# Routed experts with their remainders in halves and quarters of a block: nineteen blocks a phase instead of twenty

## The chip, the cores and the metric

The kernel runs on one core of a Trainium2 chip. The core has five engines that run side by side and meet through semaphores: TensorE (PE; its weight loads are shown apart as PEld), VectorE (DVE), ScalarE (ACT), GpSimd (POOL) and SyncE (SP), which here issues transfers. Sixteen DMA engines move data between the main memory, the on-chip memory (SBUF) and within it. TensorE writes its results to PSUM. The metric is the device time of one execution in microseconds (us), the median of several.

## The reference

Four batches of eight attention heads, whose queries are averaged in pairs, give 4 x 576 = 2304 tokens of 512 numbers. Each token goes to one of eight experts, which is a product with `w1[e]` (512 x 1024), a clip at zero, a product with `w2[e]` (1024 x 512) and a factor `p[e]`:

```python
scores = scale * np.matmul(q.reshape(B, H, S // 2, 2, D).mean(axis=3), k.transpose(0, 1, 3, 2))
attn = np.exp(scores - np.max(scores, axis=-1, keepdims=True))
x = np.matmul(attn / (np.sum(attn, axis=-1, keepdims=True) + 1e-09), v)      # then (4, 576, 512)
logits = np.einsum('bsd,de->bse', x, w_gate)
local_gate = 1.0 / (1.0 + np.exp(-np.einsum('bsd,de->bse', x, w_local).squeeze(-1)))
for s in range(S):
    fresh_e = int(np.argmax(logits[b, s]))
    e = fresh_e if s == 0 or local_gate[b, s] < 0.5 else prev_e
    prev_e = e
    h = np.maximum(x[b, s] @ w1[e], 0.0)
    out[b, s] = p[e] * (h @ w2[e])           # p: softmax of logits[b, s]
```

How many tokens an expert gets is known only when the kernel runs. With these inputs the eight experts get 192, 447, 145, 124, 34, 656, 132 and 574 tokens, which is 15 full blocks of 128 and remainders of 64, 63, 17, 124, 34, 16, 4 and 62.

## The kernel before

Attention runs in 288 steps (32 heads of nine key tiles). Behind it the last batch's tokens are routed, and then the experts run.

**Blocks.** Tokens are sorted into blocks of 128 with one expert each. There are `NST` = 20 block places `j`. An expert's remainder of more than 64 tokens takes a full block; remainders of up to 64 share the four places in `PAIRS` = (7, 11, 15, 19), two to a place, each in half of its 128 columns. A branch at the end (`tail`, L1390 on) runs further blocks where the full ones don't fit; with these inputs it is not entered.

**Phases.** All numbers are split into a high and a low float16 part, so each product is three matmuls. The weights are too large to be held at once in this form, so the experts run in eight phases of 20 blocks. An even phase multiplies every block by a quarter of `w1` (`mm1`, L1077 and `block1`, L1220: 24 matmuls of 128 columns with the weights as stationary operand; a pair takes 48 of 64 columns). An odd phase multiplies by the matching quarter of `w2` (`mm2`, L1129 and `block2`, L1231: six matmuls of 512 columns with the block as stationary operand; a pair takes twelve, two side by side in the two halves of the output). `psh` and `pso` are the outputs of the two in PSUM; ScalarE and VectorE take `hq` from `psh` (L1081, L1082), and VectorE adds `pso` to `acc` (L1144). In phase 7 each finished `acc` is written out by GpSimd with an indirect transfer (`scatter`, L1235).

**Weights.** While a phase runs, the weights of the next are loaded in 16 pieces `c` (`w_load`, L589, on SP's queue), rounded to the high part by ScalarE (`w_hi`, L594), and the low part is made by VectorE (`w_lo`, L600). The place where each piece stands in the program is a step `j` of the phase: load at `14c // 15`, high part three steps later, low part four. The first four pieces of phase 1 have buffers of their own (`we`) and are loaded at the four steps that follow attention's last.

**Copies.** In an even phase the expert's weights must be copied to a fixed place before TensorE can use them, since the expert number is a register (`copy`, L1062; L1072). VectorE makes most copies (`wc`, three buffers); those in `DMAC` are made by a transfer on SP's queue (`wd`, three buffers): eight in each even phase from phase 2 on, and the four second halves in each odd phase.

**Routing.** `gate_ops` and `route_ops` (L887 on) work out on VectorE which token stands where (`s1` to `s9`); a set of small matmuls (L940, L942) turns this into a token list `gid` per block. From `gid` GpSimd gathers the blocks' rows. The first six blocks hold tokens of the first three batches, and their work is written by hand between the routing's steps (`PLAN`).

All engines run their instructions in the order written (`manual_schedule`); SP's queue too waits at its first instruction whose buffer isn't free.

Of the kernel before, what the change touches and what calls it, by code (L numbers as in the profile page):

```python
# [448 lines left out]
NBLK = 25  # L449
NST = 20  # L450
PAIRS = (7, 11, 15, 19)
NFULL = NST - len(PAIRS)
NCOL = NBLK + len(PAIRS)
PST = slice(PAIRS[0], NST, 4)
NG = 20
# [8 lines left out]
NWD = 3  # L464
NWS = 3
NE = 4
RV = (3, 4)
# [5 lines left out]
DMAC = {5: 0, 7: 1, 9: 0, 11: 1, 13: 0, 15: 1, 17: 0, 19: 1}  # L473
NA = 14
# [5 lines left out]
def consts():  # L480
# [7 lines left out]
    full = [j for j in range(NBLK) if j not in PAIRS]  # L488
    key = np.zeros(NCOL)
    key[full] = np.arange(len(full))  # L490
    key[list(PAIRS) + list(range(NBLK, NCOL))] = len(full) + np.arange(2 * len(PAIRS))
    a[:, 384:384 + NCOL] = key[None]
    c["c16"] = a
    f = np.zeros((128, 113), np.float32)
    f[:, 0:8] = 8 - np.arange(8)
    f[:, 8:16] = np.arange(8)
    f[:, 16:32] = 1
    f[:, 24] = 0
    f[:, 34:59] = np.where(np.isin(np.arange(NBLK), PAIRS), 99, key[:NBLK])
    f[:, 60:85] = 4000 + np.arange(128)[:, None] * 25 + np.arange(25)[None]  # L500
# [23 lines left out]
class Moe:  # L524
    def __init__(self, tc, ctx, cc, io, out):
# [12 lines left out]
        self.c32 = per.tile([128, 113], F32, name="c32")  # L538
# [12 lines left out]
        self.eji = per.tile([128, NCOL], I32, name="eji")  # L551
# [3 lines left out]
        self.wcp, self.gx, self.ej, self.sl, self.ep, self.es = {}, {}, {}, {}, {}, {}  # L555
# [3 lines left out]
        self.ejf = per.tile([128, NCOL], F32, name="ejf")  # L559
# [43 lines left out]
    def gate_ops(self, b, XR, xT, sml, psum, ptag, wide):  # L603
# [185 lines left out]
        if last:  # L789
            early = [lambda: [tr(t, 6) for t in range(5)]]  # L790
            s1, s2, s3, s4, s5, s6, s7, s8, s9 = self.route_ops()
            rest = [lambda: (store(0, 512), logits(2, 3)), lambda: tr_pe(3, 0), lambda: tr_pe(3, 1), lambda: logits(3, 4), seq(tok0, o1a), r0_, lambda: o3a(0, 5), e8_, o1e, o2, seq(r1_, p1a), lambda: o3b(0, 5),
                    p1b, p1d, nop, o5, o6, s1, o6b, o7, s2, nop, p1e, s3, o7c, s4, o7d, s5, o8, s6, s7, lambda: s8(psum, ptag), s9]
            return early, lambda: logits(0, 2), rest
# [6 lines left out]
    def full_ops(self, sml, psum, ptag):  # L801
# [9 lines left out]
        def a1():  # L811
            w = self.wst.tile([128, 512], F32, name="wf", tag="wf")
            o = 0
            for k, c in (("fi", 8), ("ff", 8), ("en", 8), ("bs", 8), ("sj", n * 8), ("fs", n), ("js", n), ("m", n), ("om", n), ("ge", 200), ("e1", 25)):
                st[k] = w[:, o:o + c]
                o += c
# [45 lines left out]
        def a12():  # L862
            bj = [128, NBLK, 8]
            V.tensor_tensor(out=st["ge"], in0=c32[:, 34:59].unsqueeze(2).to_broadcast(bj), in1=st["en"].unsqueeze(1).to_broadcast(bj), op=ALU.is_ge)
# [13 lines left out]
    def route_ops(self):  # L878
# [8 lines left out]
        def s1():  # L887
# [6 lines left out]
            st["ni"], st["en"] = w[:, 216:232].bitcast(I32), w[:, 232:248]  # L894
            st["s3"] = w[:, 248:308].rearrange("p (g v) -> p g v", v=3)
            st["jf"], st["c"] = w[:, 308:328], w[:, 328:348]
            V.tensor_scalar(out=st["ni"][:, 0:8], in0=self.cy, scalar1=63.0, scalar2=None, op0=ALU.add)
            V.tensor_scalar(out=st["ni"][:, 8:16], in0=self.cy, scalar1=127.0, scalar2=None, op0=ALU.add)

        def s2():  # L900
            V.tensor_scalar(out=st["ni"], in0=st["ni"], scalar1=7, scalar2=None, op0=ALU.arith_shift_right)
            V.tensor_copy(st["vec"][:, 8:24], st["ni"])
            V.tensor_tensor(out=st["vec"][:, 16:24], in0=st["vec"][:, 16:24], in1=st["vec"][:, 8:16], op=ALU.subtract)

        def s3():
            V.tensor_tensor_scan(out=st["en"], data0=c32[:, 16:32], data1=st["vec"][:, 8:24], initial=self.F, op0=ALU.mult, op1=ALU.add)

        def s4():
            v, en = st["vec"], st["en"]
            V.tensor_tensor(out=v[:, 0:8], in0=en[:, 0:8], in1=v[:, 8:16], op=ALU.subtract)  # L910
            V.scalar_tensor_tensor(out=v[:, 16:24], in0=en[:, 8:16], scalar=float(NBLK - len(PAIRS)), in1=v[:, 16:24], op0=ALU.add, op1=ALU.subtract)
            V.tensor_tensor(out=v[:, 16:24], in0=v[:, 16:24], in1=en[:, 0:8], op=ALU.subtract)
# [15 lines left out]
        def s8(psum, ptag):  # L928
            jj, jf, en, w = st["jj"], st["jf"], st["en"], st["w2"]
            pi = st["pi"] = psum.tile([128, 512], F32, name="pi", tag=ptag)  # L930
            hg = NG // 2
            bg, bh, bj, be = [128, NG, nc_], [128, hg, nc_], [128, n, 8], [128, 8, 8]
            p2 = pi[:, 0:2 * n].rearrange("p (k j) -> p k j", k=2)
            V.tensor_tensor(out=jj[:, :, 0], in0=jf.unsqueeze(2).to_broadcast(bg), in1=c16[:, 384 + NF:384 + NCOL].unsqueeze(1).to_broadcast(bg), op=ALU.is_equal)
            for h in (1, 0):
                g = slice(h * hg, h * hg + hg)
                V.tensor_tensor(out=jj[:, g, 1], in0=jj[:, g, 0], in1=c32[:, 93 + h * hg:93 + h * hg + hg].unsqueeze(2).to_broadcast(bh), op=ALU.mult)
            for h in (1, 0):
                for g in range(h * hg, h * hg + hg):
                    T.matmul(p2, self.R[:, g], jj[:, g, :, 0:n], start=(g == hg), stop=False, skip_group_check=True)  # L940
                for g in range(h * hg, h * hg + hg):
                    T.matmul(p2[64:128, :, PAIRS[0] - NF:NST - NF:4], self.R[:, g, 0:64], jj[:, g, :, n:nc_], start=False, stop=(g == hg - 1), skip_group_check=True)  # L942
            ge, ej = w[:, 0:8 * n].rearrange("p (j e) -> p j e", e=8), self.ejf[:, NF:NBLK]
            gh, eh = w[:, 152:216].rearrange("p (j e) -> p j e", e=8), st["c"][:, 0:8]
            V.tensor_tensor(out=ge, in0=c32[:, 34 + NF:59].unsqueeze(2).to_broadcast(bj), in1=en[:, 0:8].unsqueeze(1).to_broadcast(bj), op=ALU.is_ge)
# [462 lines left out]
```

## Time and profile before

| | |
|---|---|
| median of 3 runs | 670.61 us (669.42 to 671.48) |
| the profiled execution | 671.53 us, of it 669.7 us from its first to its last instruction |
| PE, PEld busy | 644.1 us (96%), 499.6 us (75%) |
| DVE, ACT, POOL busy | 539.3 us (81%), 427.7 us (64%), 425.4 us (64%) |
| attention with the gate of the first batches | to 410 us |
| routing, first blocks and phase 0 | 410 to 471.7 us |
| phases 1 to 7 | 471.7 to 660.1 us |
| last outputs | to 669.7 us |

A busy TensorE is not one at its peak, since matmuls overlap; what a block costs is read from the start of its first matmul to the start of the next block's. Starts and durations are in us from the span's start.

### The profile page before, as it was taken

The page shows a single profiled execution, that of the slowest core. Times are in us where ns is not written, and L with a number is a line of the kernel's source. Part 1 is how long each engine was busy: PE and PEld are TensorE (multiplying, and loading weights), DVE is VectorE, ACT ScalarE, POOL GpSimd, SP SyncE. Part 2 cuts the span into 40 slices and gives each one's busy share as a digit, 9 for nine tenths or more (in the row PEclk, how much of TensorE's full clock was granted, in tenths as well). Part 3 has the DMA queues.
Part 4 walks back from the last instruction along what each step waited for, and adds up shares of the span by engine and source line. Part 5 has one row for each costly group of instructions (what it writes and reads, how often), then busy time and mean ns, then how long its engine had stood idle before and what let it go on. Part 6 is the DMA issues. An engine that isn't in the chain of part 4 may idle for free.

```text
span 669.7 us, 22907 instructions
## 1 busy us (share of the span) xinstructions
PE 644.1 (96%) x9276; PEld 499.6 (75%) x9276; DVE 539.3 (81%) x999; ACT 427.7 (64%) x852; POOL 425.4 (64%) x399
## 2 busy tenths in 40 slices
PE   7999999999999999999999998789999999999994
PEld 2587878888788888788888886778559649748941
DVE  7887897897887877888888895759559899899843
ACT  3778778777678777687777673658777435534400
POOL 8899899999899999899989758076000000000064
PEclk9999999999999999999999998999999999999998
DMA  8864654677563587563875109558669768877753
GB/s 242 203 194 137 194 153 117 185 163 166 207 185 83 165 195 144 205 195 78 202 213 135 64 2 204 208 185 268 221 218 326 269 228 294 293 265 260 280 230 118
DMA packets 83229, 128.81 MB, mean 192 GB/s; under 512 B 35759, under 2 KB 42031, under 8 KB 83120
## 3 DMA queue, kind: packets, MB, share of 16 engines
q1 hardware_dynamic: 79920, 117.24, 59.2%
q0 software_dynamic: 3200, 10.05, 4.2%
q8 instruction: 76, 1.25, 0.8%
q14 instruction: 33, 0.27, 0.1%
HBM read 68.82 MB, written 10.04 MB: 118 GB/s over the span
## 4 chain that ended last, share of the span: by engine, by line
PE 80%; DVE 9%; issue 3%; DMA 3%; POOL 2%; SPq 1%; ACT 1%; POOLq 0%; DVEq 0%; ACTq 0%
PE psh L1220 15%; PE pso L1231 14%; PE sc L272 9%; PE sc L274 9%; PE psm L246 7%; PE av L312 5%; PE av L315 5%; PE av L314 4%; PE av L316 4%; DVE mx L248 3%; DVE pl L288 2%; DMA xT<-xr 2%; PE psh L261 1%; POOL out L1235 1%; PE av L1220 1%
## 5 line engine op out<-in xcount | busy, mean ns | idle before, releaser
L276 ACT ACTIVATE ph<-sc 128x576 f32<-128x576 f32 x288 | 187.1, 653 | 85.3 <-PE sc L274 70.3
L248 DVE TENSOR_REDUCE mx<-psm 128x1 f32<-128x512 f32 (+1 forms) x300 | 194.4, 664 | 50.5 <-PE psm L246 47.3
L288 POOL TENSOR_TENSOR pl<-ph 128x576 f16<-128x576 f32 x167 | 208.9, 1266 | 7.6 <-ACT ph L276 7.6
L315 PE MATMUL av<-vt,ph 128*128 128x64 f16 x1235 | 138.7, 195 | 0.0
L314 PE MATMUL av<-vt,ph 128*128 128x65 f16 x1235 | 138.2, 192 | 0.0
L316 PE MATMUL av<-vt,pl 128*128 128x65 f16 x1235 | 137.8, 191 | 0.0
L315 PEld LDWEIGHTS <-ph 128*128 128x128 bf16 x1235 | 115.1, 97 | 20.4
L1235 POOL DMA_INDIRECT out<-acc,sid x14 | 13.7, 980 | 177.5 <-DVE acc L1144 174.9
L314 PEld LDWEIGHTS <-ph 128*128 128x128 bf16 x1235 | 116.2, 97 | 11.5 <-issue 3.6
L274 PE MATMUL sc<-qa,ks 65*128 65x288 f16 (+1 forms) x576 | 117.8, 286 | 0.0
L272 PE MATMUL sc<-qs,ks 128*128 128x288 f16 x576 | 117.5, 285 | 0.2 <-DVE st L723 0.2
L316 PEld LDWEIGHTS <-pl 128*128 128x128 f16 x1235 | 115.5, 99 | 0.0
L1231 PE MATMUL pso<-w,hq 128*128 x480 | 107.4, 380 | 0.0
L600 DVE SCALAR_TENSOR_TENSOR w<-wf,w 128x512 f16<-128x512 f32 x124 | 93.5, 759 | 13.2 <-ACT w L594 12.8
L1220 PEld LDWEIGHTS <-wc 128*128 128x128 f16 x1728 | 88.5, 99 | 4.7 <-issue 3.7
L594 ACT ACTIVATE w<-wf 128x512 f16<-128x512 f32 x124 | 76.5, 627 | 24.1 <-DMA wf<-wq 23.9
L1231 PEld LDWEIGHTS <-hq 128*128 128x128 f16 (+1 forms) x576 | 45.8, 102 | 59.8 <-issue 11.7
L1220 PE MATMUL psh<-xr,wc 128*128 128x128 f16 (+1 forms) x1584 | 84.2, 211 | 1.3 <-issue 1.0
L288 DVE TENSOR_TENSOR pl<-ph 128x576 f16<-128x576 f32 x80 | 83.8, 1047 | 0.9 <-ACT ph L276 0.9
L246 PE MATMUL psm<-ks,qs 128*128 128x512 f16 x232 | 83.4, 379 | 0.7 <-DVE mx L248 0.6
L274 PEld LDWEIGHTS <-ks 65*128 65x128 f16 (+1 forms) x576 | 56.4, 98 | 14.5
L1081 ACT ACTIVATE hq<-psh 128x256 f16<-128x256 f32 x74 | 28.5, 385 | 46.1 <-PE psh L1220 45.5
(249 smaller groups left out, 1008.4 us busy)
## 6 DMA issues: line engine op xcount, KB each, us to landing
wf<-wq SPq DMA_DIRECT2D x124, 256.0 KB
wd<-w SPq DMA_DIRECT2D x40, 512.0 KB
ks<-kd SPq DMA_DIRECT2D x32, 288.0 KB
vf<-vL SPq DMA_DIRECT2D x16, 576.0 KB
qf<-qeo SPq DMA_DIRECT2D x15, 576.0 KB
kf<-kT SPq DMA_DIRECT2D x14, 576.0 KB
qs<-qh SPq DMA_DIRECT2D x60, 72.0 KB
ks<-kl SPq DMA_DIRECT2D x30, 144.0 KB
```

The source lines that it names most:

```text
L246: T.matmul(m[:, 0:w], q[:, t * 128:t * 128 + 128], k[:, c * 512:c * 512 + w], start=True, stop=True)
L248: V.tensor_reduce(out=mx[:, i, c:c + 1], in_=m[:, 0:w], op=ALU.max, axis=AX.X)
L272: T.matmul(sc[:, c, 0:288], ksl, QS[p][:, j, c * 288:(c + 1) * 288], start=True, stop=False)
L274: T.matmul(sc[:, c, 0:288], kal, QA[p % 3][u, j, c * 288:(c + 1) * 288], start=False, stop=True)
L276: A.activation(out=PHI[g % NPH][:, r * Q:(r + 1) * Q].rearrange("p (c q) -> p c q", c=2), in_=sc[:, :, 0:288], func=AF.Exp, scale=1.0 / 16)
L288: x.tensor_tensor(out=PLO[g % NPH][:, r * Q:r * Q + Q], in0=pf, in1=top(pf), op=ALU.subtract)
L314: T.matmul(o, ph[:, c:c + 128], v[:, j, kt, 0:65], start=(kt == 0 and t == 0), stop=False, skip_group_check=True)
L315: T.matmul(o[:, 0:64], ph[:, c:c + 128], v[:, j, kt, 65:129], start=False, stop=False, skip_group_check=True)
L316: T.matmul(o, pl[:, c:c + 128], v[:, j, kt, 0:65], start=False, stop=(kt == NKT - 1 and t == 4), skip_group_check=True)
L600: self.nc.vector.scalar_tensor_tensor(out=lo, in0=t, scalar=float(2 ** (W2S if ph % 2 else W1S)), in1=hi, op0=ALU.mult, op1=ALU.subtract)
L1220: self.nc.tensor.matmul(p[:, ft, c], u[:, ws, kk, ft * 128:ft * 128 + 128], x[:, 2 * kk + xs_, c], start=(n == 0 and ft == 0 and i == 0), ...
L1231: self.nc.tensor.matmul(p[c], h(hs, ft)[:, c], u(ws, ft), start=(first and n == 0), stop=(last and n == e), skip_group_check=(m < 128))
```

## The change

- `NST` is 19. Remainders of more than 64 tokens take a full block, those of 33 to 64 a half, those of up to 32 a quarter. Pairs stand at places 8 and 13; place 18 (`QUAD`) holds four quarters of 32 columns. So an even phase has 16 full blocks, two pairs of 48 matmuls and one block of 96 matmuls with 32 columns; an odd phase has in that place 24 matmuls, four side by side. The routing has another set of 80 small matmuls (`pq`, 32 outputs each) and some more VectorE instructions.
- In phases 2, 4 and 6 ScalarE makes three of the weight copies (places 3, 10, 16; `wa`, one buffer). The transfers make eight there as before and five in an odd phase, and the quarter block's three further copies in phase 0. `wd` has four buffers. Copies by VectorE stand two blocks ahead instead of one.
- The four early pieces of phase 1 are loaded at attention's steps 240, 248, 256 and 264. Later pieces are loaded at `17c // 16 - 3`, so the first three stand in the phase before.

The core of the diff; the rest of the routing's arithmetic and the constants for it are left out.

```diff
-NST = 20
-PAIRS = (7, 11, 15, 19)
+NST = 19
+PAIRS = (8, 13)
+QUAD = 18
-NWD = 3
+NWD = 4
+ESTEPS = (240, 248, 256, 264)
-DMAC = {5: 0, 7: 1, 9: 0, 11: 1, 13: 0, 15: 1, 17: 0, 19: 1}
+DMAC = ((5, 0), (7, 0), (8, 1), (12, 0), (13, 1), (18, 1), (18, 2), (18, 3))
+ACTC = (3, 10, 16)
...
         def s3():
-            V.tensor_tensor_scan(out=st["en"], data0=c32[:, 16:32], data1=st["vec"][:, 8:24], initial=self.F, op0=ALU.mult, op1=ALU.add)
+            hq, es, ov = st["hq"][:, 9:26], st["es"][:, 0:17], st["ov"]
+            V.tensor_tensor_scan(out=es, data0=c32[:, 16:33], data1=hq, initial=0.0, op0=ALU.mult, op1=ALU.add)
+            V.scalar_tensor_tensor(out=ov[:, 9:26], in0=es, scalar=4.75, in1=hq, op0=ALU.is_gt, op1=ALU.mult)
+            V.tensor_reduce(out=st["vec"][:, 8:16].unsqueeze(2), in_=ov.rearrange("p (v e) -> p e v", v=3)[:, 0:8], op=ALU.add, axis=AX.X)
+            V.tensor_tensor_scan(out=st["en"], data0=c32[:, 85:93], data1=st["vec"][:, 8:16], initial=self.F, op0=ALU.mult, op1=ALU.add)
...
+            for g in range(NG):
+                for c in range(4):
+                    T.matmul(pq[32 * c:32 * c + 32, 0:2], self.R[:, g, 0:32], jj[:, g, :, n + 2 + c], start=(g == 0), stop=(g == NG - 1), skip_group_check=True)
...
     def positions(self, j):
-        return [j, NBLK + PAIRS.index(j)] if j in PAIRS else [j]
+        return [j, NBLK + PAIRS.index(j)] if j in PAIRS else [j, NBLK + 5, NBLK + 6, NBLK + 7] if j == QUAD else [j]
...
-        elif DMAC.get(j) == k and ph:
+        elif (j, k) in DMAC and (ph or j == QUAD):
             w, src, eng = self.wd.tile([128, 2048], F16, name="wd", tag="wd"), self.es[c], self.nc.sync.dma_start
+        elif j in ACTC and ph:
+            if c not in self.ea:
+                self.load_expert(mybir.EngineType.Activation, self.ea, c)
+            w, src, eng = self.wa.tile([128, 2048], F16, name="wa", tag="wa"), self.ea[c], lambda o, i: self.nc.scalar.activation(out=o, in_=i, func=AF.Copy)
...
-            if j in PAIRS:
-                wd = self.wcp.pop((i, 1))
-                w.append(lambda s, ft: wd[:, s * 1024 + ft * 512:s * 1024 + ft * 512 + 512])
+            for k in range(1, len(self.positions(j))):
+                wd = self.wcp.pop((i, k))
+                w.append(lambda s, ft, wd=wd: wd[:, s * 1024 + ft * 512:s * 1024 + ft * 512 + 512])
...
             copy_to(byd, min(i + 4, ph * NST + NST - 1))
-            copy_to(byv, min(i + 1, ph * NST + NST - 1))
+            copy_to(bya, min(i + 4, ph * NST + NST - 1))
+            copy_to(byv, min(i + (2 if ph else 1), ph * NST + NST - 1))
...
-                    k = j - (14 * c // 15 if ph else first[c])
+                    k, hi, lo = i - (q - 1) * NST - 17 * c // 16 + 3, 3, 4
...
-            if 0 <= s - NBH * NKT < NE:
-                m.early[s - NBH * NKT] = m.w_load(1, s - NBH * NKT)
+            if s in ESTEPS:
+                m.early[ESTEPS.index(s)] = m.w_load(1, ESTEPS.index(s))
```

SP's queue behind attention before (`xT` are the transposed tokens for the gate, `xs` the tokens' store, `vx` and `wf` other loads):

```order
L635 DMA xs<-xr 128x4x520
L635 DMA xs<-xr 64x520
L97 DMA vx_140<-vL 128x2x64
L589 DMA wf<-wq 128x512 x2
L631 DMA_TRANSPOSE xT<-xr 128x6x128 x5
L589 DMA we<-wq 128x512 x4
L635 DMA xs<-xr 128x4x512
L635 DMA xs<-xr 64x512
```

and with the change (the other two loads of `we` stand nine and five rows ahead of the first row shown):

```order
L642 DMA xs<-xr 128x4x520
L642 DMA xs<-xr 64x520
L596 DMA we<-wq 128x512
L97 DMA vx_140<-vL 128x2x64
L596 DMA we<-wq 128x512
L596 DMA wf<-wq 128x512 x2
L638 DMA_TRANSPOSE xT<-xr 128x6x128 x5
L642 DMA xs<-xr 128x4x512
L642 DMA xs<-xr 64x512
```

The `we` loads have moved from behind the transposes to ahead of them, so the transposes are followed by the store.

TensorE at a shared block of an odd phase, a pair before (`hq` is the stationary operand, `w` and `wd` the weights):

```order
L1231 MATMUL pso<-w_9473,hq 128x512
L1231 LDWEIGHTS hq
L1231 ISA
L1231 MATMUL pso<-w_9473,hq 64x512
L1231 LDWEIGHTS hq
L1231 MATMUL pso<-wd,hq 64x512
L1231 LDWEIGHTS hq
L1231 ISA
L1231 MATMUL pso<-w_9473,hq 64x512
```

and the quarter block now:

```order
L1270 MATMUL pso<-w_9559,hq 128x512
L1270 LDWEIGHTS hq
L1270 ISA
L1270 MATMUL pso<-w_9559,hq 32x512
L1270 LDWEIGHTS hq
L1270 MATMUL pso<-wd,hq 32x512
L1270 LDWEIGHTS hq
L1270 MATMUL pso<-wd,hq 32x512
L1270 LDWEIGHTS hq
L1270 MATMUL pso<-wd,hq 32x512
L1270 LDWEIGHTS hq
L1270 ISA
```

One pass over a block now has four matmuls of 32 outputs where it had two of 64.

TensorE where the routing's last matmuls end, before (`R` and `wf` place the tokens, `gvf` holds gathered rows):

```order
L942 LDWEIGHTS R
L942 MATMUL pi<-wf,R 64x2x4
L1041 LDWEIGHTS gvf
L1041 MATMUL wide<-ident,gvf 128x128
L1041 LDWEIGHTS gvf
```

and now, where 80 such loads and matmuls to `pq` follow before the first `gvf` load:

```order
L961 LDWEIGHTS R
L961 MATMUL pi<-wf,R 64x2x2
L964 LDWEIGHTS R
L964 MATMUL pq<-wf,R 32x2...
L964 LDWEIGHTS R
L964 MATMUL pq<-wf,R 32x2
L1068 LDWEIGHTS gvf
L1068 MATMUL wide<-ident,gvf 128x128
L1068 LDWEIGHTS gvf
```

The transposes of `gvf`, and all of TensorE's work behind them, have moved behind the `pq` matmuls.

## Rows read from the trace of the kernel before

**Rows 1.** The page, part 2: granted TensorE clock in 40 slices of the span.

```profile
PEclk9999999999999999999999998999999999999998
```

**Rows 2.** The chain of waits by time, experts and end: start us, us, what.

```profile
471.68 26.70 PE pso L1231 x144
498.38 27.19 PE psh L1220 x576
...
633.38 11.03 PE pso L1231 x54
...
664.17 0.97 POOL out L1235
```

**Rows 3.** Engines busy (us) in phases 2 and 3, clock, DMA share, GB/s.

```profile
498.40:525.60 27.20, 27.20 (x577) 27.11 (x578) 24.12 (x48) 16.53 (x36) 0.00 (x0) 1.00 0.92 318
525.60:552.30 26.70, 26.70 (x146) 11.42 (x145) 24.51 (x38) 9.82 (x17) 0.00 (x0) 1.00 0.70 237
```

**Rows 4.** TensorE by time in phase 2: start us, us, line, out<-in, count.

```profile
505.03 1.50 PE L1220 MATMUL psh<-xr,wd 128*128 128x128 f16 x24
506.37 1.85 PE L1220 MATMUL psh<-xr,wc 128*128 128x128 f16 x36
508.06 0.51 PE L1220 MATMUL psh<-xr,wd 128*128 128x64 f16 x12
508.41 0.51 PE L1220 MATMUL psh<-xr,wc 128*128 128x64 f16 x12
```

**Rows 5.** TensorE by time in phase 3, a pair's output block.

```profile
534.81 0.38 PE L1231 MATMUL pso<-w,hq 128*64 x1
534.81 0.38 PE L1231 MATMUL pso<-wd,hq 128*64 128x512 f16 x1
...
535.68 0.38 PE L1231 MATMUL pso<-wd,hq 128*64 128x512 f16 x1
535.99 1.47 PE L1231 MATMUL pso<-w,hq 128*128 x6
```

**Rows 6.** TensorE by time near the end of attention, a product of six columns.

```profile
404.51 0.52 PE L859 MATMUL pf<-j,R 128*128 128x6 f16 x15
404.89 0.28 PE L272 MATMUL sc<-qs,ks 128*128 128x288 f16 x1
```

**Rows 7.** Groups of ScalarE and VectorE, phase 2: busy us, mean ns, idle.

```profile
L594 ACT ACTIVATE w<-wf 128x512 f16<-128x512 f32 x16 | 9.9, 625 | 0.2 <-DMA wf<-wq 0.2
L1072 DVE COPY wc<-w 128x2048 f16 x13 | 9.0, 696 | 0.0
...
L1081 ACT ACTIVATE hq<-psh 128x256 f16<-128x256 f32 x19 | 7.3, 384 | 9.4 <-PE psh L1220 9.3
```

**Rows 8.** DMA queue in phase 2: packets, MB, share of 16 engines.

```profile
q1 hardware_dynamic: 3655, 8.56, 91.2%
```

**Rows 9.** SyncE by time behind attention.

```profile
410.11 3.44 SPq L589 DMA_DIRECT2D we<-wq  x4
```

**Rows 10.** TensorE by time behind attention.

```profile
413.80 0.86 PE L658 MATMUL psg<-wgh,xT 128*128 128x9 f16 x26 [2.38 <-DMA xT<-xr]
414.51 3.57 PE L1033 MATMUL av<-w,ident 128*128 128x512 f16 x8
```

**Rows 11.** Engines busy (us) behind attention, clock, DMA share, GB/s.

```profile
414.00:416.00 2.00, 2.00 (x29) 1.07 (x27) 2.00 (x4) 0.47 (x1) 1.69 (x2) 0.50 1.07 357
```

**Rows 12.** TensorE by time in the routing.

```profile
431.67 0.41 PE L940 MATMUL pi<-wf,R 128*128 128x38 f16 x10 [1.10 <-DVE wf L937]
...
433.19 0.90 PE L1041 MATMUL wide<-ident,gvf 128*128 128x128 f16 x8
...
439.86 0.61 PE L1033 MATMUL av<-w,ident 128*128 128x256 f16 x4 [1.31 <-issue]
```

**Rows 13.** VectorE by time in the routing.

```profile
427.01 0.18 DVE L902 CAST wf<-wf 128x16 f32<-128x16 int32 x1
427.22 0.17 DVE L903 TENSOR_TENSOR wf<-wf 128x8 f32<-128x8 f32 x1
```

## What was predicted

> **What bounds the kernel now.** First the chain of waits. From 471.68 us each phase is one row, 26.70 us for an odd phase and 27.19 us for an even one, and every such row is TensorE's own; only behind the last block is another engine the end, GpSimd with the outputs [rows 2]. Then the busy times by stretch: in phase 2 TensorE is busy for the whole 27.20 us, VectorE for 24.12 and ScalarE for 16.53; in phase 3 it is 26.70, 24.51 and 9.82 [rows 3]. So a phase lasts as long as its matmuls do while the others keep up, and VectorE has the least to spare. The clock is at full level in all slices but the one behind attention and the last [rows 1]. There, at 413.80, TensorE has waited 2.38 us for a transposed load, and the granted clock is then 0.50, the lower level [rows 10, 11]. I therefore price the experts by counting matmuls, and the stretch between 410 and 472 us apart from them.
>
> **The change part by part.**
>
> *Odd phases (1, 3, 5, 7).* In the pair's output block two matmuls start at one time, and the four passes from 534.81 to 535.68 take 0.2175 us each; the next full block starts 0.31 us behind the last pass, so the change of shape costs some 0.1 [rows 5]. From the whole phase: 20 blocks of six passes at 0.216 us are 25.92, and 26.70 less that is 0.78, or 0.195 for each of four pairs. With the change there are 19 blocks, two pairs and one quarter block: 19 x 6 x 0.216 + 3 x 0.195 = 25.2 us, 1.5 less in each of four phases, **-6.0 us**. This takes a pass of four matmuls of 32 outputs to cost what a pass of two costs. No row shows four. Two bounds: if only two ran at a time the quarter block would have twelve passes, +1.3 a phase, +5.2 in all; below, if its change of shape cost nothing, -0.8 in all. I take the row's 0.216, as two show no sign of sharing. The pair goes twofold for two matmuls. The Trainium skill ("TensorE: Matmul & The Clock Gate", section "Measured speedup vs the span model") gives 3.07 for four tiles packed by rows and 2.38 for three by columns, so less than in full for small tiles. By 3.07 the block's 24 matmuls would take 1.69 us and the phases 1.6 us more in all, an estimate from that page. The pair contradicts such a loss at two tiles; no run here shows it at four.
>
> *Even phases (2, 4, 6).* A full block is 505.03 to 506.37, 1.34 us or 55.8 ns a matmul; a pair's twelve matmuls of 64 columns take 508.06 to 508.41, 29.2 ns each, so 1.40 for 48 [rows 4]. Sixteen full blocks stay; four pairs (5.60) become two (2.80) and a block of 96 matmuls of 32 columns. Fifteen matmuls of six columns took 25.3 ns each [rows 6], so 32 columns cost between 25.3 and 29.2: 2.43 to 2.80 us; I take 2.5. That is 5.3 for 5.6, -0.3 a phase (0 to -0.4), **-0.9 us**. The place that is dropped gives nothing here: the quarter block spends it.
>
> *Phase 0.* The same -0.3, and one set of eight transposes less, 8 x 55.8 ns: **-0.75 us**. Its three transferred copies are new: 0.52 MB each, at the 318 GB/s of [rows 3] 1.65 us, 4.9 for the three, and they may go out from place 14, 5.4 us ahead of place 18. If one came late it would cost 1.6, so the bounds are -0.75 and +0.9.
>
> *Copies and loads.* At ScalarE the dearest new work is three copies of 2048 columns. It has none of that size: 128 columns more or less cost from 512 wide at 0.625 us and 256 wide at 0.384, that is 0.12 per 128 [rows 7], so 0.625 + 12 x 0.12 = 2.1 us, at most four times 0.625 = 2.5. Three make 6.3, and 16.5 + 6.3 is under the phase's 26.9; its largest waits are for TensorE, 9.4 us [rows 7]. Queued behind such a copy are one `hq` and one `w_hi`; TensorE writes on in six PSUM buffers, more than 2.1 us of blocks. The low part by VectorE and so the next phase's weights come 2 us later, of a phase's 27. VectorE gives up three copies of 0.696 us [rows 7]. On SP's queue phase 2 has 8.56 MB at 91.2% [rows 8] and stays so; an odd phase gets the quarter block's three copies for two of the pairs' four, five in place of four, so 0.70 x 26.7 plus 1.65 over 25.2 is 0.81. All of it lies beside TensorE: **0**. The cover ends where a transfer can't start in time: the last quarter copy waits for its buffer until about place 12 has been multiplied, some 17.5 us into the phase, and is wanted at 25; the loads for the next phase are queued behind it. With the fourth buffer that is 7 us for a transfer of 1.65 among others. Bounds: 0 and one such transfer late in each of three phases, +4.9.
> ScalarE as a copier: its row is 625 ns for 512 columns, VectorE's 696 for 2048 [rows 7], three and a half times dearer. The Trainium skill ("ScalarE: Activation LUTs", section "Rules for kernel authors") tells to leave such work to VectorE, up to about three times as fast in a 16-bit type; this trace agrees. By the rule the move loses 3 x 1.4 us of engine time a phase; by [rows 3] ScalarE has 10.7 us to spare and VectorE 3.1, so the sum stays at 0.
>
> *The start of phase 1's weights.* Four `we` loads stood behind the transposes and were issued at 410.11, for 3.44 us [rows 9]; they now go out at attention's steps 240 to 264 of 288, tens of us earlier. What ends at 413.80 is a transposed load that had the transfers' company. Nothing new stands between it and TensorE, so of the 2.38 us wait between none and all goes. With it might go the half clock: eight matmuls of 512 columns took 3.57 us at 414.51 [rows 10], and 8 x 0.216 is 1.73 at full clock, 1.8 less. Bounds 0 and -4.2; only part of the loads' time fell into the wait, so I take a third, **-1.4 us**.
>
> *Routing.* Three dependent steps more on VectorE at 0.21 us [rows 13]: +0.65, on the path, as TensorE's placing matmuls wait for VectorE (1.10 us at 431.67) [rows 12]. Then 80 `pq` matmuls at 25.3 ns, +2.0, ahead of the `gvf` transposes that began 1.52 us after the placing matmuls did; TensorE has 1.31 idle us shortly behind [rows 12], which they may fill: 0.7 of 2.0 remains. **+1.4 us** (0.4 to 3.4).
>
> *End.* What follows TensorE's last block, from 660.1 on, is the output chain [rows 2], and nothing in it is touched: 0.
>
> Sum: -6.0 - 0.9 - 0.75 + 0 - 1.4 + 1.4 + 0 = -7.7, so 663.8 us against the profiled execution's own 671.53 (span 669.7). The median of the runs, 670.61, is 0.92 less than that execution, so the forecast is **662.9 us**.
>
> **The rivals.**
>
> *R1, the quarter output block is less than four wide.* TensorE would stay busy and odd phases last up to 26.5 us: +1.6 to +5.2, 664.5 to 668.1. For it: no row shows four at a time. Against it: two start together and cost one pass [rows 5].
>
> *R2, the feed is late.* The quarter block's copies or the next weights miss their time, and TensorE waits at place 18 or at a phase's start. For it: a queue at 91% and VectorE at 24 of 27 us [rows 3, 8]. Against it: no such wait in any phase before, and a buffer more. Half to all of 4.9 us: 665.4 to 667.8.
>
> *R3, all of the wait behind attention goes and the clock stays up.* For it: the half clock follows the wait [rows 10, 11]. Against it: the transposes remain where they are. -4.2 in place of -1.4: 660.1.
>
> *R4, slower.* The clock falls after each quarter block, as its short matmuls give the engine little to do, and it stays low for a stretch like that at 414 us, where eight matmuls lost 1.8 us [rows 10, 11]. In eight phases that is 14.4, so 677.3; from five such stretches on the gain is gone. Against it: 48 matmuls of 64 columns four times a phase leave the clock at 1.00 [rows 3].
>
> *R5, the change doesn't do what it says.* If the remainders did not fit 19 places, the branch behind the phases would run another block, four times 1.34 and four times 1.30 at the least, +10.6: 673.5. By the counts of this input there are 16 full blocks, four remainders of 34 to 64 and three of 4 to 17, which just fit.
>
> **How the numbers follow.** Chances: forecast 0.53 (its own range 660.8 to 665), R1 0.13, R2 0.13, R3 0.15, R4 0.04, R5 0.02. A change under 0.3%, 2 us, can't be told from none here, so faster is below 668.6 and slower above 672.6. R4 and R5 are slower, 0.06; of R1 and R2 the upper ends, worst with both together, fall within 0.3%, 0.06; the rest is faster, 0.88. The range is 658.0 to 668.0: it holds R3 with some more in the even phases, and most of R1 and R2; left out are R4 and R5, the ends of R1 and R2, and the far side of R3, some 0.17.
>
> **What would show it.** In the profile of the changed kernel: odd phases of 25.2 us and even ones of 26.9, all rows of TensorE's; four matmuls to `pso` with 32 outputs starting together, passes 0.22 us apart (0.43 means R1); the 96 matmuls of 32 columns in 2.4 to 2.8 us; ScalarE's copies near 2.1 us; the wait for the transposed load under 2.4 us, and a granted clock above 0.50 behind it where R3 is right; `pq` near 2.0 us. The forecast is wrong if TensorE waits for `wd` or `w` in the phases (R2), if the clock row drops in them (R4), or if phases 1 to 7 together become shorter by less than 5 us or more than 9.

## The result and the profile after

The changed kernel took 667.15 us (median of 8), the kernel before beside it 671.37 us: ratio 0.9915, interval 0.9895 to 0.9935. It is faster, within the range of 658 to 668, but by 4.2 us (5.7 by the ratio) and not by the 7.7 forecast. A later comparison of the same two kernels gave 657.63 against 666.02 us, ratio 0.9883 (0.9854 to 0.9911). The five comparisons fell into two groups: in three the kernel before took 671 to 672 us, in two 664 to 666; so a kernel is set only against the kernel before of its own comparison.

The profiled execution took 667.72 us, its span is 665.9. The chain of waits in order of time (start, us, what), to set against [rows 2]:

```profile
474.75 25.18 PE pso L1270 x144
499.94 26.74 PE psh L1259 x576
526.67 25.18 PE pso L1270 x144
```

An odd phase has gone from 26.70 to 25.18 us, an even one from 27.19 to 26.74, and both are still one row of TensorE's. But phase 1 begins at 474.75 and not at 471.68. The busy times of phases 2 and 3 (columns as in [rows 3]):

```profile
499.90:526.70 26.80, 26.80 (x581) 26.72 (x578) 21.80 (x44) 20.39 (x38) 0.00 (x0) 1.00 0.91 315
526.70:551.80 25.10, 25.10 (x145) 10.80 (x143) 23.80 (x38) 12.15 (x19) 0.00 (x0) 1.00 0.82 283
```

VectorE is down to 21.80 us, ScalarE up to 20.39, the transfers of phase 3 up to 0.82, the clock at full level. The two quarter blocks on TensorE (start, us, line, out<-in, count), first the last 84 of the 96 matmuls of 32 columns that end phase 2, then the first side-by-side passes of the block that ends phase 3, to set against [rows 4, 5]:

```profile
524.42 1.05 PE L1259 MATMUL psh<-xr,wd 128*128 128x32 f16 x36
525.32 0.45 PE L1259 MATMUL psh<-xr,wc 128*128 128x32 f16 x12
525.62 1.05 PE L1259 MATMUL psh<-xr,wd 128*128 128x32 f16 x36
526.52 10.85 PE L1270 MATMUL pso<-w,hq 128*128 x49
...
550.38 0.40 PE L1270 MATMUL pso<-wd,hq 128*32 128x512 f16 x3
550.60 0.38 PE L1270 MATMUL pso<-w,hq 128*32 x1
550.61 0.39 PE L1270 MATMUL pso<-wd,hq 128*32 128x512 f16 x3
550.82 0.38 PE L1270 MATMUL pso<-w,hq 128*32 x1
```

Thirty-six matmuls of 32 columns take 0.90 us (524.42 to 525.32), 25.0 ns each, so 2.40 for the block. Four matmuls of 32 outputs start within 0.01 us of each other and the next four 0.22 us later: four at a time at the price of one.

Where the rest stays is to be seen behind attention, to set against [rows 10] (`psg` are the gate's products, `av<-w,ident` the warm-up matmuls, `wide<-ident,xr` the last head's transposes):

```profile
412.07 0.81 PE L665 MATMUL psg<-wgh,xT 128*128 128x9 f16 x26 [0.69 <-DMA xT<-xr]
412.73 1.89 PE L1060 MATMUL av<-w,ident 128*128 128x512 f16 x8
414.45 0.61 PE L1068 MATMUL av<-ident,gkf 128*128 128x128 f16 x8
414.90 0.17 PE L665 MATMUL psg<-wgh,xT 128*128 128x9 f16 x1
415.51 0.29 PE L665 MATMUL psg<-wgh,xT 128*128 128x9 f16 x5 [0.44 <-issue]
416.53 0.26 PE L665 MATMUL psg<-wgh,xT 128*128 128x9 f16 x4 [0.73 <-issue]
417.27 0.28 PE L665 MATMUL psg<-wgh,xT 128*128 128x9 f16 x5 [0.49 <-issue]
418.03 0.22 PE L651 MATMUL wide<-ident,xr 128*128 128x128 f16 x1 [0.48 <-issue]
418.75 0.67 PE L651 MATMUL wide<-ident,xr 128*128 128x128 f16 x9 [0.50 <-issue]
```

The wait for the transposed load is 0.69 us and not 2.38, and the eight warm-up matmuls run at full clock, 1.89 us and not 3.57: 3.4 us are won by 414.45. Then TensorE stands five times, 2.64 us in all, with nothing that the profile shows ("issue"), and what comes after that runs at the lower level of the clock. Busy times by stretch (the clock is the number behind the five engines, the last but two):

```profile
414.00:416.00 2.00, 1.36 (x17) 0.91 (x15) 1.12 (x3) 0.00 (x0) 1.70 (x2) 1.00 0.71 208
416.00:418.00 2.00, 0.53 (x9) 0.38 (x10) 0.00 (x0) 0.00 (x0) 1.68 (x4) 1.00 0.98 265
...
422.00:424.00 2.00, 2.00 (x20) 1.58 (x19) 0.39 (x1) 0.76 (x2) 0.00 (x0) 0.50 0.00 0
```

The half clock of 414 to 416 us in [rows 11] has moved to 420 to 427 us, behind a stretch in which TensorE was busy for 0.53 of 2 us. The routing's matmuls, against [rows 12]:

```profile
432.91 0.53 PE L959 MATMUL pi<-wf,R 128*128 128x36 f16 x15 [1.80 <-DVE wf L955]
...
434.66 0.79 PE L964 MATMUL pq<-wf,R 128*32 128x2 f16 x80
435.38 1.03 PE L1068 MATMUL wide<-ident,gvf 128*128 128x128 f16 x8
```

They begin 1.24 us later than before, the `gvf` transposes 2.19 later, the first block of phase 0 2.24 (447.25 against 445.01).

### The profile page after: what moved, and what is told of

Read it like the earlier page. It is cut to its first block, busy times and chain, and to the rows that moved or that the text cites. A ratio compares the mean times of both kernels' runs of the same rounds, so it can differ in the third digit from the quotient of the medians.

```text
span 665.9 us, 22923 instructions
## 1 busy us (share of the span) xinstructions
PE 638.4 (96%) x9348; PEld 498.1 (75%) x9348; DVE 528.9 (79%) x988; ACT 438.3 (66%) x855; POOL 421.6 (63%) x396
## 5 line engine op out<-in xcount | busy, mean ns | idle before, releaser
L1270 PE MATMUL pso<-w,hq 128*128 (+2 forms) x456 | 101.3, 380 | 0.0
L1270 PEld LDWEIGHTS <-hq 128*128 128x128 f16 (+2 forms) x576 | 43.6, 99 | 55.9 <-issue 7.5
L1259 PEld LDWEIGHTS <-wc 128*128 128x128 f16 x1440 | 77.2, 100 | 6.3 <-issue 5.8
L1259 PE MATMUL psh<-xr,wc 128*128 128x128 f16 (+2 forms) x1296 | 71.3, 211 | 2.9 <-ACT xr L1071 1.3
L312 PEld LDWEIGHTS av<-vx,ph 128*128 128x128 f32 x410 | 51.9, 191 | 4.8 <-issue 2.0
```

Source lines behind the costliest of these rows:

```text
L1259: self.nc.tensor.matmul(p[:, ft, c], u[:, ws, kk, ft * 128:ft * 128 + 128], x[:, 2 * kk + xs_, c], start=(n == 0 and ft == 0 and i == 0), ...
L1270: self.nc.tensor.matmul(p[c], h(hs, ft)[:, c], u(ws, ft), start=(first and n == 0), stop=(last and n == e), skip_group_check=(m < 128))
```

## The experiments

Ratios are to the kernel before in the same comparison. "First block" is the start of phase 0's first matmul to `psh`, and phase 0 lasts from there to the first matmul to `pso`: 445.01 and 26.51 us before, 447.25 and 27.35 with the change. Phases 1 to 7 are 181.1 us in the profile of every kernel below that has the nineteen blocks (181.09 to 181.19), and 188.5 to 188.6 where there are twenty; all differences lie ahead of phase 1 and in the last outputs.

| run | median us | before us | ratio | interval | first block | phase 0 |
|---|---|---|---|---|---|---|
| late_we | 668.69 | 672.37 | 0.9948 | 0.9923 to 0.9974 | 448.04 | 27.53 |
| early_we_in_before | 672.78 | 672.37 | 1.0001 | 0.9982 to 1.0020 | 446.97 | 26.79 |
| warm20 | 666.51 | 672.37 | 0.9922 | 0.9900 to 0.9944 | 446.75 | 26.07 |
| first10 | 667.60 | 672.37 | 0.9928 | 0.9907 to 0.9949 | 448.36 | 26.62 |
| gathers_late | 656.20 | 664.03 | 0.9873 | 0.9846 to 0.9899 | 440.87 | 26.34 |
| warm4 | 658.65 | 664.03 | 0.9909 | 0.9878 to 0.9940 | 442.35 | 26.48 |
| copies_on_vectore | 658.75 | 664.03 | 0.9902 | 0.9867 to 0.9938 | 441.48 | 27.28 |
| pq_4 | 656.26 | 664.03 | 0.9875 | 0.9845 to 0.9905 | 440.17 | 27.33 |
| after_again | 657.63 | 666.02 | 0.9883 | 0.9854 to 0.9911 | 439.64 | 26.03 |
| gathers_late_again | 657.66 | 666.02 | 0.9884 | 0.9845 to 0.9924 | 440.05 | 28.91 |
| gathers_late_warm4 | 658.08 | 666.02 | 0.9903 | 0.9864 to 0.9941 | 441.17 | 27.55 |
| before_again | 670.52 | 671.21 | 0.9985 | 0.9964 to 1.0006 | 443.43 | 26.47 |

**The early loads taken back.**

```diff
-ESTEPS = (240, 248, 256, 264)
+ESTEPS = (288, 289, 290, 291)
```

> The changed kernel (667.15 us) with the four early loads put back behind attention's last step; all else as changed. Theory F: the early loads save 3.4 us by 414.9 us, but TensorE then stands five times with nothing shown (2.6 us in all) and the half clock falls on 420 to 427 us in place of 413 to 420, so that by the first expert block nothing is left. F expects 666.5 to 668 us here: the transposed load awaited for about 2.4 us, the half clock at 413 to 420 as in the kernel before, no such stalls at 415 to 419, and the first block of phase 0 at 446.5 to 448.5 us. Rival G: the early loads do earn 1.7 to 3.4 us and all the loss lies in the longer routing: 669 to 670.5 us here, the first block near 449.5 to 450.5.

The ratio is 0.9948. The wait for the transposed load is 2.35 us again, the half clock stands at 416 to 426, and only one stall of over 0.25 us is left at 414 to 419 (0.45 us). The first block is at 448.04. In the traces, then, theory F holds: with and without the early loads the first block stands within 0.8 us. The median, 668.69, lies between the two theories' ranges, so this run alone leaves up to some 2 us for the loads.

**The early loads alone, in the kernel before.**

```diff
-            if 0 <= s - NBH * NKT < NE:
-                m.early[s - NBH * NKT] = m.w_load(1, s - NBH * NKT)
+            if s in (240, 248, 256, 264):
+                k = (s - 240) // 8
+                m.early[k] = m.w_load(1, k)
```

> The kernel before with one part of the change alone: the four early loads at attention's steps 240, 248, 256 and 264. Theory F (gain at the front is given back by stalls and the half clock): within 0.9 us of the kernel before, 670 to 672 us, with stalls of TensorE at 415 to 419 us and the half clock from about 420 us. Rival G (the early loads earn their part): 1.7 to 3.4 us faster, 668 to 669.6 us.

The ratio is 1.0001: theory F. TensorE behind attention in this run:

```profile
411.68 1.89 PE L1033 MATMUL av<-w,ident 128*128 128x512 f16 x8
413.40 0.83 PE L1041 MATMUL av<-ident,gkf 128*128 128x128 f16 x8
414.67 0.24 PE L658 MATMUL psg<-wgh,xT 128*128 128x9 f16 x4 [0.44 <-issue]
415.67 0.30 PE L658 MATMUL psg<-wgh,xT 128*128 128x9 f16 x6 [0.75 <-issue]
...
418.61 0.66 PE L644 MATMUL wide<-ident,xr 128*128 128x128 f16 x9 [1.12 <-issue]
```

No wait for the load at all, and the warm-up 2.8 us ahead of the kernel before; yet the last head's transposes (`wide<-ident,xr`) are through their last stall at 418.61, where the changed kernel has 418.75. The stalls, 3.3 us, took it back. So it is the early loads that bring them up, not the nineteen blocks.

**Twelve more warm-up matmuls ahead of the stalls.**

```diff
-WARMT = {0: 8, NF: 4, NF + 1: 3}
+WARMT = {0: 20, NF: 4, NF + 1: 3}
```

> The changed kernel with 20 warm-up matmuls of 512 columns in place of 8 ahead of the first gathered block: 12 more, 12 x 0.216 = 2.6 us of TensorE just ahead of the five stalls of 0.44 to 0.73 us. If the stalls are tied to the time (what TensorE lacks comes at about 418.7 us whatever it does before), the matmuls fill them: the gate's products end at about the same time, TensorE is not idle, the half clock at 420 to 427 us is gone, and the first block of phase 0 begins 0.5 to 1.5 us earlier: 665.7 to 666.7 us. If the stalls belong to the instructions, they come again behind the matmuls, and all is 2 to 2.6 us later: 669 to 669.8 us. If there are no stalls but the matmuls cost their time, 667 us.

In the trace the first answer holds:

```profile
413.27 5.85 PE L1060 MATMUL av<-w,ident 128*128 128x512 f16 x19 [0.27 <-issue]
418.96 0.61 PE L1068 MATMUL av<-ident,gkf 128*128 128x128 f16 x8
419.41 0.52 PE L665 MATMUL psg<-wgh,xT 128*128 128x9 f16 x15
```

The fifteen `psg` matmuls, spread over 2.6 us in the changed kernel, run through without a stall once they start behind 418.7. So the stalls do not belong to these instructions: what TensorE lacks is there by the time it reaches them. Whether that comes at a fixed time, or twelve large matmuls leave it the time to gather, this run alone does not tell. There is no half clock from 420 to 427, but one at 413 to 416.5 under the warm-up, and the first block comes 0.5 us earlier. The ratio, 0.9922, is not to be told from the changed kernel's 0.9915.

**The weights' pieces of phase 1 one place apart.**

```diff
-        first = [NF - 2 + c if c < NE else NF + (c - NE) * 9 // 11 for c in range(16)]
+        first = [NF - 2 + c if c < NE else NF + (c - NE) * 10 // 11 for c in range(16)]
...
-                    k, hi, lo = j - a, 2 if c >= NE else 0, 3 if c >= NE else 0
+                    k, hi, lo = j - a, 2 if c >= NE else 0, min(3, NST - 1 - a) if c >= NE else 0
```

> The changed kernel with phase 1's weight pieces spread over phase 0 as they were before (one place apart, the last low part one step earlier), so that ScalarE has two pieces ahead of a block's transposed rows once and not twice. Theory P (phase 0 is late where ScalarE's two rounded pieces in one place hold the rows and the block's outputs, the waits of 0.58 and 1.10 us at 460.5 and 465.5 us): phase 0 is 0.5 to 1.2 us shorter, 666 to 666.6 us. Rival: ScalarE's whole work bounds phase 0, or the stall at 453 to 456 us does, and the order is of no account: 667.2 us, phase 0 still 27.5 us.

The change had packed these pieces closer, which its list leaves out: twelve in ten places, where the kernel before has them in eleven and so has this run. Phase 0 is 0.7 us shorter, but its waits only change owner: 1.90 us at 461.55 and 0.54 at 465.88 are for VectorE's copies now, where the changed kernel waits 0.58 and 1.10 for ScalarE. A wait of 3.42 us ahead of phase 0 made up for the rest, and the median is 667.60. Inconclusive: warm20 has a shorter phase 0 (26.07 us) with the changed kernel's pacing.

**Four gathers later** (entries of `PLAN`; G are the gathers, T the transposes of a block, p its factors).

```diff
-d0:G0 G2;d1:G3;d2:G1;
+d0:G0 G1;
...
-c1:G4 G5 p0;
+c1:p0;
...
-c15:T1 h0 p1;
+c15:T1 h0 p1 G2 G3 G4 G5;
```

> The changed kernel with four of the six gathers that GpSimd issues behind attention (G2 to G5) put behind the gate's products and the last head's transposes; G0 and G1 stay. In six traces so far all of TensorE's 20 stalls of over 0.25 us with nothing shown, behind attention and in phase 0, stand while gathers are on their way or have just been issued. Theory C (the gathers' transfers hold up TensorE's instructions): the stalls of 2.6 us at 415 to 419 us are gone or under 0.6 us, the last head's transposes (the line of tr_pe) begin at 415.5 to 416.5 us in place of 418.0, and the routing's matmuls, 432.91 us in the changed kernel, begin 1 to 3 us earlier; the time is 664 to 666.5 us. Rival S (the store of the tokens, which runs from 414.5 to 420 us, or the place in the program): five stalls of 0.4 to 0.7 us as before, and the time 667 to 668 us.

This told nothing of the cause, since none of the four kernels of its comparison had a stall (the three others with the gathers where they were). The number of stalls in the expectation was a miscount: the six traces had 27, and with before_again it is 31 in seven; gather packets were on their way in 28 of them, which they are in most of that stretch anyway.

**Six warm-up matmuls ahead of the routing's matmuls.**

```diff
-WARMT = {0: 8, NF: 4, NF + 1: 3}
+WARMT = {0: 8, 4: 6, NF: 4, NF + 1: 3}
```

> The changed kernel with six warm-up matmuls of 512 columns (6 x 0.216 = 1.3 us) ahead of the transposes at 430.50 us, in the 1.80 us for which TensorE waits for the routing. Theory K (the clock falls at 433.7 us because of that wait, and the half clock up to 440.6 us costs the first blocks' matmuls 1.3 to 2.5 us): no half clock at 433 to 441 us, the 24 matmuls behind the gvf transposes 1.5 us long and not 2.8, the first block of phase 0 1 to 2.5 us earlier than 447.25, the time 665 to 666.3 us. Rival: the clock falls all the same, as the wait before and the short matmuls count too, or what follows waits for GpSimd's gathers and the copies and not for TensorE: 667 to 667.5 us.

What was expected of the trace came, the gain did not. TensorE here:

```profile
430.99 0.53 PE L959 MATMUL pi<-wf,R 128*128 128x36 f16 x15 [0.47 <-DVE wf L955]
...
433.65 1.50 PE L1259 MATMUL av<-xr,wc 128*128 128x128 f16 x24
...
441.79 0.62 PE L1068 MATMUL pst<-ident,gkf 128*128 128x128 f16 x8 [1.12 <-DMA gkf<-xs,gid]
442.35 0.83 PE L1259 MATMUL psh<-xr,wc 128*128 128x128 f16 x12
```

The wait for the routing is 0.47 and not 1.80, the clock stays up, the 24 matmuls take 1.50 and not 2.77 us; then TensorE waits 1.12 us for gathered rows, which it does not in after_again. From the routing's matmuls to the first block it is 11.36 us here, 11.72 there. That the six matmuls kept the clock up is not shown: gathers_late has none of them, waits as long as the changed kernel, and has the 24 matmuls in 1.50 us too, with the clock at 1.00 from 410 to 442 us:

```profile
428.93 0.53 PE L959 MATMUL pi<-wf,R 128*128 128x36 f16 x15 [1.78 <-DVE wf L955]
...
431.59 1.50 PE L1259 MATMUL av<-xr,wc 128*128 128x128 f16 x24
```

So the wait for the routing alone does not bring the lower level. Nor does the full clock bring the first block earlier there: it begins 11.94 us behind the routing's matmuls, after a wait of 1.71 us for gathered rows.

**The three copies back on VectorE.**

```diff
-ACTC = (3, 10, 16)
+ACTC = ()
```

> The changed kernel with the three copies of phases 2, 4 and 6 on VectorE in place of ScalarE. By the forecast these copies lie beside TensorE on either engine: phases 2, 4 and 6 stay at 26.74 us each and the time at 667.2 us (within 0.6 us); VectorE is then busy for 23 to 25 of a phase's 26.7 us. Rival: VectorE does not keep up with three copies more (3 x 0.69 us a phase), TensorE waits for its copies, and the even phases become 0.5 to 2 us longer: 668.7 to 673 us.

Phases 2, 4 and 6 are as long as with ScalarE's copies, 26.65 us each from their first matmul to the next phase's first; phase 2, then its copies here and in the changed kernel (busy us, mean ns, idle before):

```profile
493.90:520.60 26.70, 26.70 (x577) 26.57 (x574) 23.60 (x47) 15.89 (x35) 0.00 (x0) 1.00 0.93 323
```

```profile
L1103 DVE COPY wc<-w 128x2048 f16 x13 | 8.9, 682 | 2.9 <-PE psh L1259 2.9
```

```profile
L1103 DVE COPY wc<-w 128x2048 f16 x10 | 6.9, 691 | 0.0
L1097 ACT ACTIVATE wa<-w 128x2048 f16 x3 | 5.7, 1907 | 0.9 <-ACT hq L1112 0.9
```

VectorE's copies still wait 2.9 us for TensorE, so it keeps up. The move to ScalarE gains and costs nothing; this part of the change could be left out. (The median, 658.75, has runs from 654 to 665 in it and says no more.)

**The routing's matmuls to `pq`, four of 80.** The quarter block then finds only some of its tokens.

```diff
-            for g in range(NG):
-                for c in range(4):
-                    T.matmul(pq[32 * c:32 * c + 32, 0:2], self.R[:, g, 0:32], jj[:, g, :, n + 2 + c], start=(g == 0), stop=(g == NG - 1), skip_group_check=True)
+            for c in range(4):
+                T.matmul(pq[32 * c:32 * c + 32, 0:2], self.R[:, 0, 0:32], jj[:, 0, :, n + 2 + c], start=True, stop=True, skip_group_check=True)
```

> The changed kernel with 4 of the routing's 80 matmuls to pq: the quarter block then finds only some of its tokens, and its rows of the output are left out. The 80 took 0.72 us at half clock, ahead of the gvf transposes. If they lie on the path (as forecast, at 0.7 us), the first block of phase 0 begins 0.6 to 0.9 us earlier than 447.25 and the time is 666.2 to 666.7 us. Rival: the wait of 1.00 us at 442.6 us takes them up, and the time stays at 667.2 us.

From the routing's first matmul to the `gvf` transposes it is 1.62 us here (428.96 to 430.58) and 2.20 in after_again (427.92 to 430.12); from there to the first block 9.59 and 9.52. The 80 matmuls lie on the path for 0.6 us. Against the changed kernel of its own comparison there is no median, so the absolute expectation isn't tested.

**The changed kernel again, the late gathers again, and both edits.**

> The changed kernel itself, as the control for the runs beside it: where TensorE's five stalls at 415 to 419 us are there, 666.5 to 668 us and 0.991 to 0.992 of the kernel before; where they are not (as in the four runs of the earlier call, whose kernel before took 664.0 us and whose first expert block began at 440 to 442 us), 657 to 659 us and 0.987 to 0.991.

> The kernel with four gathers late, once more, since no kernel of its first call showed the stalls that it was to test, so that it told nothing of their cause. Beside a control that shows the stalls: theory C (the gathers' transfers hold up TensorE's instructions) expects under 0.6 us of stalls at 415 to 419 us and 1 to 3 us less than the control; rival S (the store of the tokens, or the place in the program) expects the stalls and the time of the control within 0.8 us. Beside a control without stalls both expect the control's time within 0.8 us.

> Both edits at once, the four gathers late and six warm-up matmuls ahead of the transposes before the routing's matmuls. If the late gathers remove stalls and the warm-up matmuls the half clock at 433 to 441 us, the gains add: 2 to 4 us less than the control where it has stalls, 1 to 2 us less where it has none (there warm4 alone had its routing's matmuls to phase 1 in 37.8 us, the kernel without it 39.1). If one cause is behind both, no more than the better of the two alone: within 0.8 us of the run with late gathers.

None of the three has a stall, so theories C and S are not told apart. The late gathers are the control's equal (0.9884 against 0.9883), and both edits together, 0.9903, add nothing: the two with late gathers wait 2.74 and 2.55 us for a copy of VectorE's within phase 0. No kernel tried is clearly better than the changed one. The control itself is the more telling, TensorE behind attention in after_again:

```profile
412.47 1.89 PE L1060 MATMUL av<-w,ident 128*128 128x512 f16 x8
414.19 0.61 PE L1068 MATMUL av<-ident,gkf 128*128 128x128 f16 x8
414.64 0.52 PE L665 MATMUL psg<-wgh,xT 128*128 128x9 f16 x15
415.02 0.72 PE L651 MATMUL wide<-ident,xr 128*128 128x128 f16 x10
```

and the stretch behind it there, then in the changed kernel's first profile:

```profile
420.00:428.00 8.00, 5.24 (x95) 4.98 (x96) 7.38 (x39) 5.98 (x13) 0.15 (x2) 1.00 0.45 164
```

```profile
420.00:428.00 8.00, 7.25 (x88) 6.38 (x89) 4.64 (x23) 3.63 (x6) 0.44 (x3) 0.57 0.35 133
```

The same program passes the same place without a stall, has the clock at 1.00 where the first profile has 0.57, and begins phase 0 at 439.64 us, 7.6 earlier. Its phase 0 is 1.3 us shorter and its end 3.3, which makes 12.2 us of the span between two profiles of one program.

**The kernel before again.**

> The kernel before itself, profiled once more, to have its trace from a run without the stalls. In the last two calls it took 664 to 666 us, and the changed kernel 657.6, without stalls and with its first expert block at 439.64 us. If the stalls of TensorE explain why the change brought 4.2 us in the first comparison and 8.4 in the last, the kernel before shows here no stall with nothing shown, the wait of about 2.4 us for the transposed load and the half clock behind it as ever, its first expert block at 440 to 442.5 us, phase 0 of 26.0 to 26.6 us and phases 1 to 7 of 188.6 us. If instead the kernel before is slower there by its front, its first block stands at 443 us or later. If the run shows stalls as the first profile did: first block near 445 us, 670 to 672 us.

The last answer holds as to the time and the stalls (four, in the routing and phase 0, none at 415 to 419); the first block, 443.43, is 1.6 us ahead of the first profile. A trace of the kernel before without stalls is not to be had from these runs.

## Why the prediction was right, and where it was wrong

- **Odd phases** (-6.0): 26.70 to 25.18 us, four times, -6.1. The pass of four at the price of one is a row now, and R1 is out. By the 3.07 that the Trainium skill ("TensorE: Matmul & The Clock Gate", section "Measured speedup vs the span model") gives for four tiles packed by rows, a phase would have been 25.6 us, an estimate. That figure does not carry over to these four tiles packed by columns, with the full 128 rows of contraction, for which the section has none: 25.18 was measured.
- **Even phases** (-0.9): -1.4. The mechanism holds; mis-sized is the quarter block, 2.40 us for the 2.5 taken and just under the lower bound of 2.43. The rest is the little by which a phase exceeds its rows' sum: 27.19 for 27.04 before, 26.74 for 26.64 now.
- **Copies and loads** (0): phases 1 to 7 are all TensorE's, R2 and R4 are out there. A copy on ScalarE takes 1.91 us where 2.1 were estimated, 2.8 times VectorE's 0.69 and not three and a half times.
- **The start of phase 1's weights** (-1.4): this step failed. It priced the wait and the half clock behind it, and took what is won there to be won at the end. 3.4 us were won, more than I dared to take, and lost again within the next 11 us: 2.64 to the stalls, the rest to the half clock at 420 to 427 us. At the five small matmuls to `pc` (424.89 before, 425.01 after) nothing is left. early_we_in_before shows it with nothing else changed, in a comparison with the stalls; what the early loads bring without the stalls no run tells. R3's condition, that the clock stays up behind attention, was met only in runs without stalls.
- **Routing** (+1.4): from `pc` to the `gvf` transposes +2.1 us in the first profile: 0.67 for VectorE's added steps (0.65 forecast), some 0.4 for transposes at half clock ahead of them, 0.95 for the placing matmuls and `pq`. The 80 took 0.72 us, 9 ns each, not 25.3: mis-sized, and what should have filled an idle 1.31 us lay on the path.
- **Phase 0** (-0.75): +0.84 in the first profile. The step that failed is the count itself: I counted TensorE's matmuls, as in the phases behind. But here ScalarE also takes each block's transposed rows, and in the first profile it sets the end over several blocks. Its chain there:

```profile
459.14 0.39 ACT hq L1112
459.53 0.91 ACT xr L1071
460.44 0.52 ACT w L601
460.96 0.27 ACT hq L1112
461.23 0.92 ACT xr L1071
462.15 1.03 ACT w L601 x2
```

  Rows, outputs and one piece are 0.92 + 0.28 + 0.52 = 1.72 us a block, beside TensorE's 1.34 + 0.45 = 1.79, and two pieces in a place are 2.2. A block fewer of TensorE's gives nothing while ScalarE has its twelve pieces to round, in ten places where it had eleven. How much of that is the pacing isn't settled: over all traces with the nineteen blocks phase 0 lasted 26.03 to 28.91 us.
- **End** (0): 9.6 us became 10.2 in the first profile, and it is 6.9 in after_again. In the first profile VectorE begins the addition for place 13 at 652.71, 3.7 us after TensorE's last matmul of that block has ended (649.00); in after_again it begins at once, at 640.11.

Together, in the first profile: -7.5 in the phases, +2.24 and +0.84 ahead of them, +0.54 at the end, -3.8 of the span. In the comparison of after_again, the change brought 8.4 us, near to the sum of 7.7; of what terms it is made up no trace tells, since there is none of the kernel before without stalls. In the first comparison the forecast of 662.9 missed by 4.3 us: ahead of phase 1 a gain of 0.75 was forecast, and a loss of 3.1 came. The range reached to 668 because of R1 and R2, and neither came; that 667.15 lies within it is luck in this part.

What stays open: why TensorE stands there, and why in some comparisons not at all. The runs show that the stalls end at 418.6 to 418.9 us in four kernels whatever came before, that large matmuls fill them, and that they come and go with the comparison. Whether the gathers, the store of the tokens or something else holds the instructions up they do not show; leaving the store out wasn't tried. Three things narrow it. The chip does not tell the two groups of comparisons apart: the one numbered 4 had one of either, with the kernel before at 672.4 and at 666.0 us. No load of instructions ends the stalls: the queues that carry such loads (q8 and q14) move nothing in the first profile between 412.2 and 426.0 us, and the stalls there are over at 418.75. And it is not TensorE alone. VectorE too begins late there, 1.2 us after the product that it takes (`av`) has ended at 411.29:

```profile
412.51 0.17 DVE L1356 TENSOR_SCALAR rc<-av 128x5 f32<-128x5 f32 x1 [1.89 <-PE av L312]
```

In after_again it begins at 411.09, 0.04 us after the product's end, and the store of the tokens goes out at 413.14 and not at 414.55.

## What to carry to other kernels

In a stretch where one engine is the end for the whole of it, count its instructions by rows and the sum holds to a few tenths of a microsecond. A microsecond won ahead of a chain of small dependent steps is not yet won: ask what stands at the next place, what the clock does there, and try the edit alone in the old kernel. Before counting on a shorter stage, add up the second engine's work per block too: in phase 0 ScalarE's 1.72 us beside TensorE's 1.79, and 2.2 where two pieces met in a place, were enough for it to set the end.

## What the runs showed of the hardware

- Four matmuls of 32 outputs and 512 columns, side by side in the output, take one pass of 0.22 us.
- 80 matmuls of two columns and 32 outputs, four side by side, took 0.70 to 0.72 us, 9 ns each, where matmuls of six columns and 128 outputs took 25.3.
- TensorE stood 0.3 to 1.3 us at a time with nothing that the profile shows, 31 times in seven traces and never in seven others of nearly the same programs; at 415 to 419 us it ran some eight to ten instructions (matmuls and weight loads) between two stalls. Two profiles of one program, with and without, begin phase 0 7.6 us apart; what part of this is the stalls', the half clock's behind them and VectorE's late start is not shown.
- Behind the same wait of TensorE's for the routing (1.8 us) the granted clock fell to 0.50 in the changed kernel (434 to 440 us) and stayed at 1.00 in gathers_late.
